# Retention by pairs of 64-token chunks, every product 64x64, in a kernel of retention and two mixtures of experts

## Chip, cores and metric

The kernel runs on one core of a Trainium2 chip. The metric is the device time of one execution in microseconds, a median of several runs. Engines are called as in the profile: PE is TensorE's matmul, PEld its weight load, DVE is VectorE, ACT ScalarE, POOL GpSimd, SP the queue that issues most DMAs.

## What is computed

Three layers. The first is retention over 4 sequences of 576 tokens with 8 heads of 64; the second a dense layer with softplus; the third a mixture of 8 experts, two per token.

```python
# q, k, v: (4, 8, 576, 64)
scores = scale * np.matmul(q, k.transpose(0, 1, 3, 2))
gamma = 1.0 - 2.0 ** (-5.0 - np.arange(H))
Dmat = np.where(rel >= 0, gamma[:, None, None] ** rel[None, :, :], 0.0)
ret = np.matmul(scores * Dmat, v)            # -> x: 2304 tokens x 512
h = x @ w_in                                 # 512 -> 2048
x = (np.maximum(h, 0) + np.log1p(np.exp(-np.abs(h)))) @ w_out
...
# top-2 gating over 8 experts, each 512 -> 1024 -> 512
```

## The kernel before

The 2304 tokens are cut into 18 chunks of 128 (C), of which 9 (PAIR) make two sequences; the fifth of nine straddles a border. Retention runs chunk by chunk (c), all in f32, from inputs that are laid out for it: `qk` has q and k with the head's dimension on the partitions (heads 2j and 2j+1 in the two halves, ROW), `kv` has k and v with the tokens on the partitions. For each chunk:

- `att_load` (L213) issues the DMAs of `qk` and `kv`, for the first ones also of the constants: `cm` (masks with decay, 512 KB), `ck` (decay for k), `CQ` (decay for q).
- `att_scale` (L226) multiplies k (L231) and q (L235) by their decay, on POOL but for chunk 0.
- `att_qk` (L237): eight products of 64x128x128 into two tiles `pa` (L243), one for each half of the rows of the array, and two multiplications by the mask on DVE (L247).
- `att_kv` (L252): eight products with 64 output rows (L262), and the new state on DVE, copied or added (L266, L268).
- `att_av` (L270): eight products with the old state (L281) and eight with the masked scores (L286) into one tile `px`; ACT writes its f16 part scaled into `x1` (L293), DVE the remainder (L294). Three chunks make a tile of 384 tokens for the next layer.

The dense layer takes f16 in two parts, three products for one. `g1` (L300) makes 128 columns of the hidden layer, 12 products of 128x384 (L306), evacuated by ACT (L315, L316) and softplus; `g2` (L325) multiplies by the second matrix (L337). Its weights come as f64: `decode` (L132) turns them into f32 on ACT (L141, L152) and DVE (L153, L155), `parts` (L159) splits them into two f16 parts on ACT (L161) and POOL (L162). 16 pieces are so treated.

The order of the work in the first part is a list written out by hand, `START` (L789): W is `warm` (products on a constant tile while the first inputs load), A load, S scale, Q, K, V the three attention steps, L a piece's load, a its decode, b its split, g one step of g1 or g2. The later chunks are put at steps of g1 by a small table (L769): loads 8 steps ahead of step g0, scaling 4 ahead, `att_qk` at g0, `att_kv` and `att_av` at g0+2. A scheduler then sets the order on every engine; each engine runs its own list in order.

In the same stage the experts' weights are read (L352, L354), split on ACT (L361) and DVE (L362) and written back to memory (L366), 64 pieces of 512 KB; each engine's list mixes them with the rest. After some 455 us follow the expert blocks (L683, L711), which the change does not touch.

## Time and profile before

| | |
|---|---|
| median of 3 runs | 912.62 us (911.99 to 914.01) |
| the profiled execution | 914.52 us, of which the profile's span is 912.3 us |
| PE busy | 885.7 us, 97% of the span |
| PEld, DVE, ACT, POOL busy | 50%, 72%, 42%, 29% |
| mean clock granted to PE | 0.988 of full |

The page gives busy time by engine, the span in 40 equal slices of 22.8 us with the busy share in tenths, the granted clock and the DMA's share and rate. Further views of the trace group instructions by line, list them in order of time, name who waited for whom, and give the busy time by stretch. A matmul on f32 stands in the trace as two passes, each with its own weight load, so eight written products count x16. A pass's own time is longer than the distance to the next, since passes overlap; what counts is the distance of starts.

### The profile page before, as it was taken

How to read it: one execution, taken by the hardware profiler on the slowest of the kernel's cores; microseconds unless marked ns; L12 is line 12 of the kernel's file. 1: busy time of each engine (PE TensorE's matmuls, PEld its weight loads, DVE VectorE, ACT ScalarE, POOL GpSimd, SP SyncE). 2: the span in 40 equal slices, each digit the busy share in tenths (PEclk: the TensorE clock that was granted, in tenths of full speed). 3: DMA queues.
4: the chain of work that ended last, by engine and by line, in shares of the span. 5: the costliest groups of instructions: out<-in, count | busy, mean ns of one | idle time of the engine just before them, and what ended most of it. 6: DMA issues, size and time to landing. Idle time of an engine off the chain costs nothing. (4 is left out here: it accounts for less than half of the span.)

```text
span 912.3 us, 17461 instructions
## 1 busy us (share of the span) xinstructions
PE 885.7 (97%) x5466; PEld 459.5 (50%) x5466; DVE 654.2 (72%) x1367; ACT 383.4 (42%) x595; POOL 260.5 (29%) x239
## 2 busy tenths in 40 slices
PE   7789999999999999999999999999999999999996
PEld 6554555555555555555544444444444444444442
DVE  4687866886887975434636789778887788878880
ACT  2589975775766674435432122221222212222120
POOL 1666642501410320110412423222232222321112
PEclk8899999999999999999999999999999999999998
DMA  9848999999999994003286875976357856875412
GB/s 352 318 170 271 296 283 394 384 318 351 388 336 342 376 403 121 1 1 70 67 242 128 139 122 101 240 189 156 66 152 176 208 126 163 246 178 157 116 24 35
DMA packets 141096, 187.11 MB, mean 205 GB/s; under 512 B 80016, under 2 KB 89232, under 8 KB 138960
## 3 DMA queue, kind: packets, MB, share of 16 engines
q1 hardware_dynamic: 130512, 164.90, 57.6%
q0 software_dynamic: 10496, 21.05, 11.8%
q8 instruction: 53, 0.87, 0.4%
q14 instruction: 35, 0.29, 0.1%
HBM read 246.01 MB, written 54.20 MB: 329 GB/s over the span
## 5 line engine op out<-in xcount | busy, mean ns | idle before, releaser
L702 DVE STREAM_TRANSPOSE ht<-hr 32x256 f32<-32x256 f32 x608 | 265.1, 436 | 11.7
L683 PE MATMUL ph<-w,xt 128*128 x984 | 218.9, 379 | 1.4 <-DMA xt<-xr 1.4
L711 PE MATMUL py<-w,ht 128*128 x984 | 218.6, 379 | 0.0
L306 PE MATMUL pg<-x,wi 128*128 128x384 f16 x1152 | 203.6, 326 | 2.7 <-POOL wi L162 1.9
L337 PE MATMUL p<-w,g 128*128 128x512 f16 x864 | 202.3, 381 | 1.7 <-POOL w L162 1.7
L306 PEld LDWEIGHTS <-wi 128*128 128x128 f16 x1152 | 111.4, 98 | 87.0 <-POOL wi L162 3.4
L683 PEld LDWEIGHTS <-xt 128*128 128x128 f16 x984 | 96.1, 98 | 117.2 <-DMA xt<-xr 1.6
L711 PEld LDWEIGHTS <-ht 128*128 128x128 f16 x984 | 96.3, 98 | 116.1
L723 POOL DMA_INDIRECT out_dram<-y,ti x41 | 64.9, 1583 | 279.0 <-ACT y L722 259.4
L337 PEld LDWEIGHTS <-g 128*128 128x128 f16 x864 | 82.6, 98 | 95.2 <-issue 6.2
L688 ACT ACTIVATE hr<-ph 128x512 f16<-128x512 f32 x82 | 60.0, 734 | 157.2 <-PE ph L683 150.4
L689 DVE SCALAR_TENSOR_TENSOR hr<-ph,hr 128x512 f16<-128x512 f32 x82 | 59.2, 727 | 66.3 <-ACT hr L688 65.2
L722 ACT ACTIVATE y<-py,ti 128x512 f32<-128x512 f32 x41 | 28.2, 687 | 180.4 <-PE py L711 180.4
L362 DVE SCALAR_TENSOR_TENSOR w<-w 128x1024 f16<-128x1024 f32 x64 | 79.0, 1236 | 32.4 <-ACT w L361 30.3
L320 DVE SCALAR_TENSOR_TENSOR r<-a,r 128x768 f32<-128x768 f32 x48 | 56.1, 1169 | 55.1 <-ACT a L319 54.2
L515 POOL DMA_INDIRECT table<-tb,pos x36 | 44.7, 1243 | 156.7 <-DVE pos L500 124.2
L361 ACT ACTIVATE w<-w 128x1024 f16<-128x1024 f32 x64 | 67.4, 1053 | 50.6 <-DMA w<-in_moe_w_dram 31.8
L315 ACT ACTIVATE r<-pg 128x384 f32<-128x384 f32 x96 | 46.7, 486 | 84.7 <-PE pg L306 84.6
L660 POOL DMA_INDIRECT xr<-X,ti x41 | 43.4, 1057 | 20.7 <-POOL ti L657 10.2
L316 ACT ACTIVATE a<-pg 128x384 f32<-128x384 f32 x96 | 46.6, 486 | 0.0
L318 ACT ACTIVATE a<-a 128x768 f32<-128x768 f32 x48 | 40.5, 843 | 1.1
L319 ACT ACTIVATE a<-a 128x768 f32<-128x768 f32 x48 | 40.3, 841 | 0.9
(132 smaller groups left out, 596.7 us busy)
## 6 DMA issues: line engine op xcount, KB each, us to landing
w<-wsc SPq DMA_DIRECT2D x78, 2048.0 KB
w<-in_moe_w_dram SPq DMA_DIRECT2D x64, 512.0 KB
wsc<-w SPq DMA_DIRECT2D x64, 512.0 KB
qk<-in_qk_dram SPq DMA_DIRECT2D x18, 512.0 KB
kv<-in_kv_dram SPq DMA_DIRECT2D x18, 512.0 KB
w<-in_moe_w_in_dram SPq DMA_DIRECT2D x8, 1024.0 KB
w<-in_moe_w_out_dram SPq DMA_DIRECT2D x8, 1024.0 KB
out_dram<-zero SPq DMA_DIRECT2D x1, 4608.0 KB
```

What stands on the lines that cost most here:

```text
L306: nc.tensor.matmul(pg, lhsT=wi[:, a, k, f * P:(f + 1) * P], rhs=x[:, b, k, :], start=n == 0, stop=n == 11)
L315: LAST["relu"] = nc.scalar.activation(r[:, i], pg, AF.Relu, scale=S_G / sx)
L320: nc.vector.scalar_tensor_tensor(out=r, in0=a, scalar=S_G, in1=r, op0=ALU.mult, op1=ALU.add)
L337: m = nc.tensor.matmul(PG[t, j], lhsT=g[:, a, f % 2, j * P:(j + 1) * P], rhs=wo[b][:, f, :], start=f == 0 and a + b == 0, stop=f == NFB - ...
L361: nc.scalar.activation(h[:, 0], t, AF.Copy, scale=s)
L362: nc.vector.scalar_tensor_tensor(out=h[:, 1], in0=t, scalar=s, in1=h[:, 0], op0=ALU.mult, op1=ALU.subtract)
L683: M1[i].append(nc.tensor.matmul(ph, lhsT=xt[:, a * 4 + k, :], rhs=AR[0][:, ds(r * 8192 + (b * 4096 + k * 1024 + n * 512), 512)], start=m = ...
L688: LAST["act"] = nc.scalar.activation(hi, ph, AF.Relu)
L689: nc.vector.scalar_tensor_tensor(out=lo, in0=ph, scalar=0.0, in1=hi, op0=ALU.max, op1=ALU.subtract)
L702: nc.vector.transpose(dst[32 * f:32 * f + 32, :, t], src[32 * t:32 * t + 32, :, f])
L711: M2[i].append(nc.tensor.matmul(py, lhsT=ht[:, c, :, a], rhs=AR[1][:, ds(r * 8192 + (b * 4096 + c * 512), 512)], start=len(M2[i]) == 0, st ...
L723: LAST["pool"] = nc.gpsimd.indirect_dma_start(out=out[:, :], out_offset=bass.IndirectOffsetOnAxis(ap=ti[:, 1:2], axis=0), in_=y[:, :], in_ ...
```

## The change

A chunk of 128 tokens is now a pair of 64-token chunks (x = 0, 1), nine of them to a sequence, so no chunk straddles a border. Every product is 64x64 with a contraction of 64, and uses a quarter of TensorE's array: rows `ROW[p]`, columns by where the output lies. The inputs are reordered on loading so that in each half of the partitions lies, for head half r, the chunk x = p ^ r. Decay moves: v is multiplied once by gamma to the minus position (`att_scale`, one operation), scores are only masked by a triangle of ones (one multiplication of 128x512, `tri`), states are plain sums, and the output is multiplied by gamma to the position, the scale and S_X1 (two multiplications into `f`, by `UP`). `f` lies in SBUF; ACT makes the f16 part from it, and the remainder is taken by DVE for the first three chunks and by POOL after.

`att_in` joins the scores and the two chunks' states in one group of up to 32 products; `att_out` the outputs, up to 32. Each group's products are issued together (`issue_after`). Both row halves of the array write to the one tile `pa`, and to the one tile `pst`, on different halves of the partitions. For each chunk DVE now has one mask, up to four state steps of 64x256 and two multiplications of 128x256. The constants are 68 KB (`cd`) ahead of the first `kv` and five pieces of `UP`, of up to 256 KB, one after each of the first five chunks. The warming is 22 products of 128x128 in place of 6 and 64 small ones.

```diff
@@ -49,31 +49,34 @@
...
+    up = g.T[None, :, None, :, None] ** (HALF * n[:, None, None, None, None] + t) * (S_X1 / np.sqrt(D))
...
+            down[p, :, :, r] = g[None, None, :, r] ** -(HALF * k[None, :, None] + t[:, None, None])
...
+        "c_down": np.concatenate([
+            np.tile(t[:, None] <= t[None, :], (2, 1)), down.reshape(P, PAIR * 8)], axis=1).astype(np.float32),
...
+    def units(a):
+        a = a.transpose(0, 2, 1, 3).reshape(NCH, 2, HALF, 4, 2, D)
+        return np.stack([np.stack([a[:, p ^ r, :, :, r] for r in range(2)], axis=1) for p in range(2)], axis=1)
...
@@ -186,113 +189,105 @@
     def warm(n):
         pw = ps.tile([C, 4, C], F32, tag="p2", name="pw", bufs=3)
-        for i in range(6):
+        for i in range(n):
             nc.tensor.matmul(pw[:, i % 4, :], lhsT=heat, rhs=heat, start=True, stop=True)
...
-            r, w = i // 2 % 2, HALF if i % 32 < 20 else C
-            nc.tensor.matmul(pw[r][ROW[i % 2], i // 4 % 4, :w], lhsT=heat[ROW[r], :64], rhs=heat[ROW[r], :w], start=True, stop=True)
...
+    UP = view(1, 12288, [PAIR, 4, HALF], F32)
+    cd = view(1, 29696, [HALF + PAIR * 8], F32)
+    tri, down = cd[:, :HALF], cd[:, HALF:].rearrange("p (n g) -> p n g", n=PAIR)
+    LD, AA, ST, X1 = {}, {}, {}, {}
+    def kinds(c):
+        return [(2 * c + x) % PAIR for x in range(2)]
     def att_load(c):
...
+        qk = ap.tile([P, 2, 8, HALF], F32, name="qk", bufs=3)
         nc.sync.dma_start(out=qk, in_=ins["qk"][c])
         if c == 0:
...
+            nc.sync.dma_start(out=cd, in_=ins["c_down"])
+        kv = ap.tile([P, 2, 8, D], F32, name="kv", bufs=3)
         nc.sync.dma_start(out=kv, in_=ins["kv"][c])
...
+        if c < 5:
+            n = 2 * c
+            m = min(n + 2, PAIR)
+            nc.sync.dma_start(out=UP[:, n:m], in_=ins["c_up"][:, n:m])
         LD[c] = (qk, kv)
     def att_scale(c):
         qk, kv = LD[c]
...
         e = nc.vector if c < 1 else nc.gpsimd
...
+        e.tensor_tensor(out=kv[:, 1], in0=kv[:, 1], in1=down[:, c % PAIR, :, None].to_broadcast([P, 8, D]), op=ALU.mult)
+    def att_in(c, tag="pa"):
         qk, kv = LD[c]
...
+        ka, kb = kinds(c)
+        pool, n = (ps, 3) if tag == "p2" else (ps1, 2)
+        pa = pool.tile([P, 8, HALF], F32, tag=tag, name="pa", bufs=n)
+        pst = pool.tile([P, 8, D], F32, tag=tag, name="pst", bufs=n)
+        use = (ka < PAIR - 1, kb < PAIR - 1)
+        with ExitStack() as tied:
+            for j in range(4):
+                for r in range(2):
+                    g = r * 4 + j
+                    for p in range(2):
+                        x = p ^ r
+                        if use[x]:
+                            m = nc.tensor.matmul(pst[ROW[1 - p], x * 4 + j], lhsT=kv[ROW[p], 0, g], rhs=kv[ROW[p], 1, g],
+                                                 start=True, stop=True)
+                            if LAST.get("in") != c:
+                                LAST["in"] = c
+                                tied.enter_context(tc.issue_after(m.ins))
+                        nc.tensor.matmul(pa[ROW[p], g], lhsT=qk[ROW[p], 1, g], rhs=qk[ROW[p], 0, g], start=True, stop=True)
+        a = AA[c] = ap.tile([P, 8, HALF], F32, name="a", bufs=2)
+        nc.vector.tensor_tensor(out=a, in0=pa, in1=tri[:, None, :].to_broadcast([P, 8, HALF]), op=ALU.mult)
+        sa = ST.get(2 * c)
+        for x in range(2):
+            if not use[x]:
+                continue
+            st = ST[2 * c + x + 1] = ring(("st", x), 1, 21504 + x * 2048, [4, D], F32, 2)
+            old = ST.get(2 * c + x)
             for r in range(2):
...
+                y = ROW[1 - r ^ x]
+                add = pst[y, 4 * x:4 * x + 4]
+                if (ka, kb)[x] == 0:
+                    nc.vector.tensor_copy(st[y], add)
+                else:
+                    nc.vector.tensor_tensor(out=st[y], in0=old[ROW[r ^ x]], in1=add, op=ALU.add)
+    def att_out(c, tag="pa"):
+        (qk, kv), a = LD.pop(c), AA.pop(c)
+        pool, m = (ps, 3) if tag == "p2" else (ps1, 2)
+        px = [pool.tile([P, 4, HALF], F32, tag=tag, name="px", bufs=m) for x in range(2)]
+        kk = kinds(c)
+        seen = set()
+        parts = [(True, j, 1 - x, r) for j in range(4) for x in range(2) for r in range(2) if kk[1 - x]]
+        mine = [(False, j, x, r) for j in range(4) for x in range(2) for r in range(2)]
+        with ExitStack() as tied:
+            both = parts + mine if kk[1] else mine + parts
+            end = {(x, r): n for n, (i, j, x, r) in enumerate(both)}
+            for n, (inter, j, x, r) in enumerate(both):
+                p, g = x ^ r, r * 4 + j
+                m = nc.tensor.matmul(px[x][ROW[r], j], lhsT=ST[2 * c + x][ROW[p], j] if inter else kv[ROW[p], 1, g],
+                                     rhs=qk[ROW[p], 0, g] if inter else a[ROW[p], g],
+                                     start=(x, r) not in seen, stop=end[x, r] == n, skip_group_check=True)
+                if not seen:
+                    tied.enter_context(tc.issue_after(m.ins))
+                seen.add((x, r))
+        f = ring("f", 1, 25600, [4, 2, HALF], F32, 2)
+        for x in range(2):
+            nc.vector.tensor_tensor(out=f[:, :, x], in0=px[x], in1=UP[:, kk[x]], op=ALU.mult)
         T, i = c // 3, c % 3
         if i == 0:
             X1[T] = mp1.tile([P, 2, KC, TT], F16, tag="x1", name="x1", bufs=2)
...
+        hi, lo = (X1[T][:, b, :, i * C:(i + 1) * C] for b in range(2))
+        f = f.rearrange("p j x t -> p j (x t)")
+        nc.scalar.activation(hi, f, AF.Copy)
+        e = nc.vector if c < 3 else nc.gpsimd
+        e.tensor_tensor(out=lo, in0=f, in1=hi, op=ALU.subtract)
     G, PG, X2R, LAST = {}, {}, {}, {}
@@ -770,9 +765,8 @@
         g0 = max({7: 22, 8: 27}.get(c, 0), (c // 3 - 1) * NS + (-1, 4, 9)[c % 3])
         at((1, max(12, g0 - 8)), att_load, c)
         at((1, max(16, g0 - 4)), att_scale, c)
-        at((1, g0), att_qk, c)
-        at((1, g0 + 2), att_kv, c)
-        at((1, g0 + 2), att_av, c)
+        at((1, g0), att_in, c)
+        at((1, g0 + 2), att_out, c)
     for t in range(NTILE - 1):
         at((2, (t + 1) * NS + 2), logits, t)
         at((2, (t + 1) * NS + (6 if t < NTILE - 2 else 3)), ranks, t)
@@ -787,9 +781,9 @@
     START = """
-        W64 A0 L A1 S0 Q0 K0 L A2 S1 V0 Q1 K1 a L A3 S2 V1 b Q2 K2 a L A4 S3 V2 b a L b g g
-        Q3 K3 a L A5 S4 V3 b g g a L b g g Q4 K4 a L S5 V4 b g g Q5 K5 a L V5 L b g g a L b g g
-        a L b g g a L b g g a L b g A6 g a L b g g a L b g g S6 a b g g Q6 a b g K6 g a V6 b r
+        W6 W16 A0 L A1 S0 Q0  L A2 S1 V0 Q1  a L A3 S2 V1 b Q2  a L A4 S3 V2 b a L b g g
+        Q3  a L A5 S4 V3 b g g a L b g g Q4  a L S5 V4 b g g Q5  a L V5 L b g g a L b g g
+        a L b g g a L b g g a L b g A6 g a L b g g a L b g g S6 a b g g Q6 a b g  g a V6 b r
         g g g g
     """.split()
     PA, PB = 2, 2
@@ -828,8 +822,8 @@
             piece(s)
         else:
             c = int(s[1:])
-            f = {"A": att_load, "S": att_scale, "Q": att_qk, "K": att_kv, "V": att_av, "W": warm}[s[0]]
-            f(c, "p2") if s[0] in "KV" and c < 3 else f(c)
+            f = {"A": att_load, "S": att_scale, "Q": att_in, "V": att_out, "W": warm}[s[0]]
+            f(c, "p2") if s[0] == "V" and c < 3 else f(c)
     while order:
         step()
     for g in sorted(todo):
```

On PE the list shows chunk 16's two groups, between the wide products of `g1` (L306 before, L301 now). Before, the scores, and later the state and output:

```order
L306 MATMUL pg<-x_2754,wi 128x384
L243 MATMUL pa<-qk 128x128 x8
L306 LDWEIGHTS wi
```

```order
L306 MATMUL pg<-x_2754,wi 128x384
L262 MATMUL pst<-kv 64x64 x8
L281 MATMUL px<-w_85 64x128 x8
L286 MATMUL px<-a,kv 64x128 x8
L442 LDWEIGHTS w_85
```

Now (L239 the states, L244 the scores in turn, 16 of each; then L274 the output, with the old state and with the scores):

```order
L301 MATMUL pg<-x_3112,wi 128x384
L239 MATMUL pst<-kv 64x64
L244 MATMUL pa<-qk 64x64
L239 MATMUL pst<-kv 64x64
L244 MATMUL pa<-qk 64x64
```

```order
L301 MATMUL pg<-x_3112,wi 128x384
L274 MATMUL px<-qk,w_85 64x64 x16
L274 MATMUL px<-a,kv 64x64 x16
L437 LDWEIGHTS w_85
```

The state's products have moved from the second group into the first, between the scores.

On ACT the first rows of the program, before (L141 and L152 decode, L161 the first f16 part of a piece, L293 a chunk's output into `x1`):

```order
L141 ACTIVATE w_84<-w_84 128x1024
L152 ACTIVATE low<-w_84 128x512
L293 ACTIVATE x_246<-px 128x4x128
L152 ACTIVATE low<-w_84 128x512
L293 ACTIVATE x_246<-px 128x4x128
L141 ACTIVATE w_84<-w_84 128x1024
L152 ACTIVATE low<-w_84 128x512
L161 ACTIVATE wi<-w_85 128x4x256
L152 ACTIVATE low<-w_84 128x512
L293 ACTIVATE x_246<-px 128x4x128
L161 ACTIVATE wi<-w_85 128x4x256
```

Now (L144, L155, L164 and L288 in the same roles):

```order
L144 ACTIVATE w_84<-w_84 128x1024
L155 ACTIVATE low<-w_84 128x512 x2
L288 ACTIVATE x_225<-w_85 128x4x128
L164 ACTIVATE wi<-w_85 128x4x256
L144 ACTIVATE w_84<-w_84 128x1024
L155 ACTIVATE low<-w_84 128x512 x2
L288 ACTIVATE x_225<-w_85 128x4x128
L164 ACTIVATE wi<-w_85 128x4x256
L144 ACTIVATE w_84<-w_84 128x1024
L155 ACTIVATE low<-w_84 128x512 x2
L288 ACTIVATE x_225<-w_85 128x4x128
L164 ACTIVATE wi<-w_85 128x4x256
```

The first two pieces' f16 parts now each stand ahead of the next chunk's output, where both stood behind the second and the third; three pieces are decoded before the first wide product where it was two.

## Rows read from the trace of the kernel before

**Rows 1.** The page: PE's busy time, and its busy tenths by slice.
```profile
PE 885.7 (97%) x5466; PEld 459.5 (50%) x5466; DVE 654.2 (72%) x1367; ACT 383.4 (42%) x595; POOL 260.5 (29%) x239
...
PE   7789999999999999999999999999999999999996
```

**Rows 2.** Busy time by stretch: us; PE, PEld, DVE, ACT, POOL; clock, DMA share, GB/s.
```profile
33.00:107.00 74.00, 67.76 (x502) 38.10 (x501) 57.36 (x83) 66.51 (x103) 49.57 (x32) 0.98 0.73 236
105.00:245.00 140.00, 140.00 (x1057) 80.06 (x1056) 108.77 (x182) 95.16 (x151) 42.63 (x27) 1.00 1.04 353
245.00:345.00 100.00, 100.00 (x758) 57.56 (x757) 79.31 (x120) 68.67 (x105) 22.75 (x19) 1.00 1.01 360
345.00:450.00 105.00, 105.00 (x716) 58.24 (x714) 49.24 (x144) 46.54 (x87) 12.89 (x13) 1.00 0.17 41
```

**Rows 3.** ACT's waits from 105 to 345 us: total us, times, longest.
```profile
ACT w L361 <- DMA w<-in_moe_w_dram: 31.8, 23, 4.9
ACT r L315 <- PE pg L306: 21.9, 23, 3.2
ACT w L361 <- DMA wsc<-w: 17.2, 12, 6.1
```

**Rows 4.** PE in order of time, chunk 16: start us, us from first start to last end.
```profile
352.12 1.16 PE L243 MATMUL pa<-qk 64*128 64x128 f32 x16
353.21 2.12 PE L306 MATMUL pg<-x,wi 128*128 128x384 f16 x12
...
361.10 0.69 PE L262 MATMUL pst<-kv 128*64 128x64 f32 x16
361.62 1.05 PE L281 MATMUL px<-w 128*64 128x128 f32 x16
362.49 1.04 PE L286 MATMUL px<-a,kv 128*64 128x128 f32 x16
363.47 1.06 PE L442 MATMUL lg<-wg,w 128*128 128x16 f16 x36
```

**Rows 5.** Busy time by stretch, as rows 2: the warming's quarter passes, the start.
```profile
6.20:6.23 0.03, 0.03 (x12) 0.03 (x8) 0.00 (x0) 0.00 (x0) 0.00 (x0) 1.00 1.10 426
6.20:6.70 0.50, 0.50 (x44) 0.50 (x40) 0.00 (x0) 0.00 (x0) 0.00 (x0) 1.00 1.02 351
12.70:19.50 6.80, 6.70 (x58) 5.95 (x60) 3.87 (x8) 1.13 (x2) 2.27 (x2) 0.50 1.04 396
27.20:32.70 5.50, 4.79 (x48) 4.31 (x49) 1.52 (x3) 0.56 (x2) 1.16 (x1) 0.50 1.03 395
```

**Rows 6.** Line 194's passes from 6.35 to 6.70 us: ns shortest/median/longest, first, last start.
```profile
L194 PE MATMUL pw<-heat x36: 218/218/218, 6.2 to 6.7; 64*64 64x64 f32 x36
```

**Rows 7.** DVE in order of time, the start.
```profile
10.96 0.85 DVE L266 COPY w<-pst 64x256 f32<-64x256 f32 x2
...
32.77 0.69 DVE L294 SCALAR_TENSOR_TENSOR x<-px,x 128x512 f16<-128x512 f32 x1 [2.85 <-ACT x L293]
35.26 1.29 DVE L153 SCALAR_TENSOR_TENSOR low<-w,low 128x512 int32<-128x512 int32 x2 [1.79 <-ACT low L152]
```

**Rows 8.** POOL in order of time, the start, and chunk 16's scaling.
```profile
14.09 1.04 POOL L231 TENSOR_TENSOR kv<-kv,ck 128x512 f32<-128x512 f32 x1 [11.03 <-DMA kv<-in_kv_dram]
15.09 1.27 POOL L235 TENSOR_TENSOR w<-qk,w 128x512 f32<-128x512 f32 x1
24.00 2.13 POOL L162 TENSOR_TENSOR wi<-w,wi 128x1024 f16<-128x1024 f32 x1 [7.65 <-ACT wi L161]
...
296.39 1.19 POOL L231 TENSOR_TENSOR kv<-kv,ck 128x512 f32<-128x512 f32 x1 [6.65 <-DMA kv<-in_kv_dram]
```

**Rows 9.** PE in order of time, the warming.
```profile
1.15 2.93 PE L190 MATMUL pw<-heat 128*128 128x128 f32 x12 [1.15 <-DVE heat L91]
4.01 3.52 PE L194 MATMUL pw<-heat 64*64 64x64 f32 x128
```

**Rows 10.** ACT in order of time, the third piece's f16 part.
```profile
38.05 1.06 ACT L161 ACTIVATE wi<-w 128x1024 f16<-128x1024 f32 x1
```

More of the change, by code (lines that the diff above doesn't have):

```diff
@@ L227, in att_scale @@
         qk, kv = LD[c]
-        u = c % PAIR
         e = nc.vector if c < 1 else nc.gpsimd
-        if u < PAIR - 1:
-            e.tensor_tensor(out=kv[:, 0], in0=kv[:, 0], in1=ck[:, kind(c), :, None].to_broadcast([C, H, D]), op=ALU.mult)
-        if u:
-            n = HALF if u == 4 else C
-            QS[c] = ring("qs", 1, 24576, [4, C], F32, 2)
-            e.tensor_tensor(out=QS[c][:, :, :n], in0=qk[:, 0, :, :n], in1=CQ[kind(c)][:, :, :n], op=ALU.mult)
-    def att_qk(c):
-        qk, kv = LD[c]
-        pa = [ps1.tile([C, 4, C], F32, tag="pa", name="pa", bufs=2) for g in range(2)]
-        for j in range(4):
-            for g in range(2):
-                nc.tensor.matmul(pa[g][:, j, :], lhsT=qk[ROW[g], 1, j, :], rhs=qk[ROW[g], 0, j, :], start=True, stop=True)
-        AA[c] = []
-        for g in range(2):
-            a = ap.tile([C, 4, C], F32, name="a", bufs=2)
-            nc.vector.tensor_tensor(out=a, in0=pa[g], in1=cm[:, g], op=ALU.mult)
-            if c % PAIR == 4:
-                nc.gpsimd.memset(a[:HALF, :, HALF:], 0.0)
-            AA[c].append(a)
@@ L252, in att_kv @@
-    def att_kv(c, tag="pa"):
-        qk, kv = LD[c]
-        u = c % PAIR
-        if u == PAIR - 1:
-            return
-        pst = ps.tile([P, 4, D], F32, tag=tag, name="pst", bufs=3) if tag == "p2" else \
-            ps1.tile([P, 4, D], F32, tag="pa", name="pst", bufs=2)
-        for j in range(4):
-            for r in range(2):
-                nc.tensor.matmul(pst[ROW[r], j], lhsT=kv[:, 0, 2 * j + r], rhs=kv[:, 1, 2 * j + r], start=True, stop=True)
-        st = ST[c + 1] = STZ[c % 2]
-        for r in range(2):
-            if u in (0, 4):
-                nc.vector.tensor_copy(st[ROW[r], r], pst[ROW[r]])
-            else:
-                nc.vector.tensor_tensor(out=st[ROW[r], r], in0=ST[c][ROW[r], r], in1=pst[ROW[r]], op=ALU.add)
@@ L270, in att_av @@
-    def att_av(c, tag="pa"):
-        (qk, kv), qs, a = LD.pop(c), QS.pop(c, None), AA.pop(c)
-        u = c % PAIR
-        px = ps.tile([P, KC, C], F32, tag=tag, name="px", bufs=3) if tag == "p2" else \
-            ps1.tile([P, KC, C], F32, tag="pa", name="px", bufs=2)
-        n, last, w = 0, 15 if u else 7, HALF if u == 4 else C
-        for j in range(4 if u else 0):
-            for r in range(2):
-                nc.tensor.matmul(px[ROW[r], j, :w], lhsT=ST[c][:, r, j], rhs=qs[:, j, :w], start=n < 2, stop=False,
-                                 skip_group_check=True)
-                n += 1
-        for j in range(4):
-            for r in range(2):
-                nc.tensor.matmul(px[ROW[r], j, :], lhsT=kv[:, 1, 2 * j + r], rhs=a[r][:, j], start=n < 2, stop=n >= last - 1,
-                                 skip_group_check=True)
-                n += 1
+        e.tensor_tensor(out=kv[:, 1], in0=kv[:, 1], in1=down[:, c % PAIR, :, None].to_broadcast([P, 8, D]), op=ALU.mult)
@@ new lines, in att_in @@
+    def att_in(c, tag="pa"):
+        qk, kv = LD[c]
+        ka, kb = kinds(c)
[5 more added lines that the diff above has]
+            for j in range(4):
+                for r in range(2):
+                    g = r * 4 + j
+                    for p in range(2):
+                        x = p ^ r
[14 more added lines that the diff above has]
+            old = ST.get(2 * c + x)
+            for r in range(2):
+                y = ROW[1 - r ^ x]
[4 more added lines that the diff above has]
+                    nc.vector.tensor_tensor(out=st[y], in0=old[ROW[r ^ x]], in1=add, op=ALU.add)
@@ L291, in att_av @@
             X1[T] = mp1.tile([P, 2, KC, TT], F16, tag="x1", name="x1", bufs=2)
-        x = X1[T]
-        nc.scalar.activation(x[:, 0, :, i * C:(i + 1) * C], px, AF.Copy, scale=S_X1)
-        nc.vector.scalar_tensor_tensor(out=x[:, 1, :, i * C:(i + 1) * C], in0=px, scalar=S_X1,
-                                       in1=x[:, 0, :, i * C:(i + 1) * C], op0=ALU.mult, op1=ALU.subtract)
+        hi, lo = (X1[T][:, b, :, i * C:(i + 1) * C] for b in range(2))
[3 more added lines that the diff above has]
+        e.tensor_tensor(out=lo, in0=f, in1=hi, op=ALU.subtract)
     G, PG, X2R, LAST = {}, {}, {}, {}
```

44 lines of the change are left out of this document (9 added, 35 removed).

## Prediction

> **What bounds the kernel now.** I read the page's head first [rows 1]: TensorE (PE) is busy for 97% of the span, so what shortens PE's work should shorten the kernel, unless something else is nearly as full. It holds stage by stage. In the slices PE is below nine tenths only in the first three and in the last one. The table of stretches [rows 2] splits what lies between: from 105 to 345 us PE is never idle, but the DMA queues are just as full (share 1.04 and 1.01, 353 and 360 GB/s); from 345 to 450 PE is full and the DMA at 0.17. From 33 to 107 PE has 67.8 of 74 us, and ACT 66.5: while the first layer's weights are decoded, two engines are nearly full. ACT's waits in the middle stretch [rows 3] say what the DMA does there: the splitting of the second layer's weights (L361) stands still for 31.8 us on loads and 17.2 us on stores, in front of the activations that PE's products wait for; PE has so far always had enough buffered. So: a start bound by chains of waits, a decode stage bound by ACT and PE, a stage in which PE is the bound with the DMA right behind it, and PE alone after that.
>
> **The retention on PE, per chunk.** Chunk 16 shows the old price [rows 4]: scores from 352.12 to the next line's 353.21, 1.09 us; state and output from 361.10 to 363.47, 2.37 us, of which the state takes 0.52 (361.10 to 361.62) and the product with the old state 0.87. Sum 3.46 us. Each written product is two passes in the trace (eight give x16). The new code has 32 products of 64x64 in each of two groups, 64 passes each. The trace of before has this very shape in its warming: over a stretch of 0.47 us with a pass long 0.218 us, the table counts 44 passes where its first 0.03 us counts 12, so 32 passes start in 0.47 us, **14.6 ns** a pass [rows 5, 6]; the quarters are used in turn there as here. A group then takes 63 x 14.6 ns and one pass's own 0.218 us until the wide products go on: 1.14 us. Two groups: 2.28 us, **1.18 us less** per full chunk. Upper bound for a pass: the state's rows, 16 in 0.52 us, 33 ns, where only two parts of the array work side by side; lower bound half of 14.6, as no row shows passes nearer. I take 14.6, since array shape, width and alternation are the same.
>
> After 105 us lie chunks 7 to 17. Seven are full: 8.3. Chunks 8 and 17 make no state (2.94 before): 0.66 each. Chunk 9 reads none (2.59): 0.3. Chunk 13 multiplies half as many columns by the old state (3.03): 0.75. Together **10.6 us**, 8.8 of them before 345 us and 1.8 behind it.
>
> **How much of the 8.8 arrives.** The bytes of that stage do not change (the new chunk loads are as large; only the constants shrink, early on). 240 us at some 356 GB/s must fit into 231 us: 371 GB/s. Where the queues are full without a break, at the start, the rows show 395 and 396 [rows 5]. It fits on average, at 94% instead of 90%. But ACT stands still on DMA for 49 us of 240 already, and at these places PE's lead is used up first. Bounds: nothing lost, or all 8.8. I take a third, 2.9, off: 5.9 arrive.
>
> **The other engines in that stage.** DVE loses one masking product of 0.68 us and the remainder (0.69), and gets two additions of 64x256 (0.42 each) and two half products of the output with the decay (bounded by the same 0.42 from below and 0.68 from above): 0.3 to 0.8 us a chunk, 3 to 9 us in 188 of 240 us busy [rows 2, 7]; hidden, as PE is never idle and so no wait of PE for DVE stands in that stage. POOL swaps the scaling of q (1.27 us) for the remainder, of half the size of the decode's 2.13 us, 1.07: about equal [rows 8]. ACT's evacuation has the same size. The first group now waits for POOL's scaled values where the old scores did not. That is hidden: scaled values lie ready tens of us ahead (chunk 16's at 297.6, its scores at 352.12 [rows 4, 8]).
>
> **The start.** Warming: 22 products of 128 instead of 6 and 64 small ones. Six took 2.86 us (from 1.15 to 4.01) [rows 9], so 22 take 10.5 us if the clock stays low and half of that if it were high throughout: they end between 6.4 and 11.6. Either way chunk 1 comes later: its values landed at 14.09 [rows 8], and with 0.46 MB less of mask constants and 0.26 MB of output decay ahead of them some 0.2 MB earlier, 0.5 us at 396 GB/s: 13.6. The clock: from 12.7 to 19.5 and from 27.2 to 32.7 it is at the lower level, 0.50 (1.2 GHz) [rows 5], after PE had stood idle; the new groups leave more gaps, so I take 0.50 throughout, doubling a group to 2.1 us. From there, with the pitches of DVE's rows (0.6 us for 128x512, 0.42 for 64x256) [rows 7]:
> - POOL scales until 14.6; group one until 16.7; mask and two state steps, 1.5: 18.2; group two until 20.3; two products with the decay, 0.85: 21.2; behind them stand two pairs of decode steps and a remainder, 3.0: 24.2.
> - Chunk 2's group one is long done; mask and state 1.5: 25.7; group two: 27.8; products 0.85: 28.7; two decode steps and the remainder, 1.85: **30.5**.
>
> Only then does the first layer have both parts of its input. Before, the remainder ended at 33.46 [rows 7]: 2.9 us won. It would be 6 more if the clock stayed high. On ACT the order moves too: the first decoded piece now goes ahead of chunk 1's evacuation (the order shows it), and the third piece, at 38.05 before [rows 10], follows at about 30.5 + 1.2 = 31.7: **6 us** earlier. In the decode stage ACT is 90% busy, so 6 us of ACT's lead last to its end if nothing else binds; PE, with 2.9 and four chunks of 1.18, is ahead by 7.6. The smaller holds: 6 us. Bounds: 2.9 (PE's lead alone, chunks swallowed by waits) and 10 (clock up early, and idle gaps closing).
>
> **Sum.** 6 + 5.9 + 1.8 = 13.7 us. The profiled execution took 914.5 us (span 912.3), 1.9 above the median of 912.62; 914.5 less 13.7 is 900.8, and at the level of the median **898.9**. After 450 us nothing changes; that part moves earlier as a whole.
>
> **Rivals.**
> - *The DMA holds the middle.* Splitting, loads and stores keep their pace, and PE, faster, waits for ACT behind L361. For it: share 1.0 and ACT's 49 us. Against it: ACT also waited 21.9 us for PE in the same stretch [rows 3], so the DMA was not the pace everywhere. Then 6 + 1.8 arrive: 904.8.
> - *Everything arrives.* The clock rises early in the start (10) and the DMA gives way (8.8 + 1.8): 892.
> - *The halves take turns, and it is slower.* In the new groups the upper and the lower half of the array's rows write one bank of PSUM (`pa`, and `pst`) in the same moment, on different partitions; in the old warming, and in the old scores, each row half had a bank of its own, so no row shows this pattern. If the halves have to take turns, a pass costs 29.2 ns, a group 2.06 us, a full chunk 4.1 instead of 3.46. It decides from 24 ns a pass on, where two groups cost as much as the old chunk. Loss after 105 us: seven at 0.66, and some 2.7 for the four others, 7.3 us. The start's chain gets four groups longer by 1.9 us at the low clock, which takes its gain: 920. For it: even with separate banks the old scores' two row halves took 68 ns a pass (16 in 1.09 us), so halves do not always run freely side by side. Against it: within a bank they write different partitions.
>
> The Trainium skill (TensorEngine Tiling (Array Packing), section "Gotcha 1: PSUM Pressure") says that different row tiles cannot access the same PSUM bank simultaneously and that software must see to it; by that rule this rival would be the forecast. Its page PSUM — Partial Sum Buffer (section "PSUM bank collisions raise a hardware error") says of two engines that different quadrants of one bank run clean. No row here shows either.
>
> **How the numbers follow.** Forecast 0.55 (its own range 894 to 905: the start giving between 2.9 and 9, the DMA taking between a sixth and two thirds); DMA holds 0.20; everything 0.12; turns 0.13. What a measurement can tell from no change is 0.2%, 1.8 us. The first three are faster, with 0.02 taken off for starts that lose what PE gains; in the fourth a little falls within 0.2%. Faster 0.85, same 0.03, slower 0.12. The range from 890 to 907 takes in the first three and leaves out the fourth with the tails.
>
> **What would show it.** Right: 64 passes of a group starting within about 0.93 us between 105 and 450 us, a group about 1.1 us from its first start to the next line's; the first wide product near 30 us; the third decoded piece near 32 us; PE idle of a few us in all between 105 and 345 us, named as waiting for ACT behind L361 or for its chain. Wrong: passes at 29 ns (turns); ACT behind L361 waiting on the DMA as long as before while PE stands idle some 9 us (DMA); first wide products after 33 us.

## The result, and the profile after

The changed kernel takes **919.73 us** (918.38 to 921.6, 4 runs) against 912.33 for the kernel before, measured beside it: ratio 1.0079, 95% interval 1.0057 to 1.0101. It is slower by 0.8%; 898.9 was predicted. The profiled execution took 919.36 us.

The page's head, and below it the table of stretches (columns as in [rows 2]), which answer to [rows 1, 2]:

```profile
PE 878.6 (96%) x6458; PEld 450.7 (49%) x6458; DVE 668.8 (73%) x1402; ACT 383.7 (42%) x595; POOL 256.1 (28%) x232
...
PE   7878999999999999899999999999999999999996
```

```profile
33.00:107.00 74.00, 64.37 (x674) 36.21 (x673) 58.31 (x87) 63.92 (x99) 44.70 (x27) 0.95 0.75 253
105.00:345.00 240.00, 233.73 (x2377) 130.87 (x2376) 193.30 (x313) 163.04 (x253) 64.36 (x45) 0.99 1.00 350
345.00:450.00 105.00, 101.62 (x822) 55.45 (x821) 49.49 (x130) 45.56 (x85) 14.94 (x15) 0.98 0.15 35
```

PE is busy 7 us less, and the kernel is longer: from 105 to 345 us PE stands idle for 6.3 us where it was never idle, from 345 to 450 for 3.4, and its clock is below full in both stretches. What PE waited for, over the span (us in total, times, longest):

```profile
PE px L274 <- DVE w L259: 10.7, 9, 2.0
...
PE px L274 <- issue: 2.6, 5, 1.1
```

The first row is the second group of a chunk (L274) waiting for the state additions on DVE (L259); in the last, "issue" means that nothing in the trace explains the wait.

The passes themselves came as forecast. PE in order of time, chunk 16, to be held against [rows 4]:

```profile
351.02 0.27 PE L239 MATMUL pst<-kv 64*64 64x64 f32 x1
...
352.11 2.12 PE L301 MATMUL pg<-x,wi 128*128 128x384 f16 x12
...
360.00 0.69 PE L274 MATMUL px<-qk,w 64*64 64x64 f32 x32
360.52 0.65 PE L274 MATMUL px<-a,kv 64*64 64x64 f32 x32
361.10 1.06 PE L437 MATMUL lg<-wg,w 128*128 128x16 f16 x36
```

The groups take 1.09 and 1.10 us, 2.19 against 3.46 before. So PE does its work faster and then stands. To see where the time is lost, I count `g1`'s passes (12 to a step of the first layer) and take the start of the first one of a step, in us, in each profiled execution; the last three columns are experiments of the next section:

| step | before | changed | prio | prioall | rank3 |
|---|---|---|---|---|---|
| 0 | 32.8 | 28.6 | 29.0 | 29.0 | 29.5 |
| 6 | 62.8 | 54.9 | 54.9 | 53.1 | 55.2 |
| 12 | 91.8 | 90.6 | 90.6 | 88.4 | 90.9 |
| 66 | 342.3 | 341.2 | 335.0 | 333.7 | 335.2 |
| 78 | 396.9 | 399.7 | 395.3 | 393.9 | 387.6 |
| 90 | 444.7 | 447.5 | 443.1 | 441.7 | 435.5 |
| end of span | 912.3 | 917.5 | 912.2 | 907.7 | 902.5 |

The changed kernel leads by 4.2 us at the start and 7.9 at step 6, by 1.2 at step 12, by 1.1 at step 66, and is 2.8 us behind at step 78. Three places, then: steps 6 to 12, the middle stage, where the 8.8 us that PE's work was forecast to shrink by left no trace, and steps 66 to 78. Behind step 90 another 2.4 us go (2.8 us behind there, 5.2 at the end).

**The middle stage.** DVE in order of time around chunk 14, whose first group had ended at 300.8:

```profile
304.75 1.23 DVE L357 SCALAR_TENSOR_TENSOR w<-w 128x1024 f16<-128x1024 f32 x1 [0.25 <-ACT w L356]
306.01 0.42 DVE L259 TENSOR_TENSOR w<-w,pst 64x256 f32<-64x256 f32 x1
306.47 0.69 DVE L246 TENSOR_TENSOR a<-pa,w 128x512 f32<-128x512 f32 x1
307.26 0.96 DVE L315 SCALAR_TENSOR_TENSOR r<-a,r 128x768 f32<-128x768 f32 x1
308.25 0.41 DVE L259 TENSOR_TENSOR w<-w,pst 64x256 f32<-64x256 f32 x1
308.70 0.56 DVE L316 CAST g<-r 128x768 f16<-128x768 f32 x1
309.29 0.42 DVE L259 TENSOR_TENSOR w<-w,pst 64x256 f32<-64x256 f32 x1
309.72 0.96 DVE L318 TENSOR_TENSOR g<-r,g 128x768 f16<-128x768 f32 x1
310.69 0.42 DVE L259 TENSOR_TENSOR w<-w,pst 64x256 f32<-64x256 f32 x1
```

and PE at the same time:

```profile
308.88 0.33 PE L274 MATMUL px<-qk,w 64*64 64x64 f32 x4
311.17 0.62 PE L274 MATMUL px<-qk,w 64*64 64x64 f32 x26 [1.95 <-DVE w L259]
```

The four additions are 1.7 us of work, spread over 5.1 us of DVE's list among the softplus (L315, L316, L318), behind a splitting (L357) that itself waits for ACT. The second group reads the state after the chunk's first half, and writes its `px` into the two buffers that `pa` and `pst` held, so it cannot finish before the last addition. Between 110 and 375 us PE's waits for these additions add up to 5.9 of 6.3 us of idle time.

**Steps 66 to 78.** PE in chunk 17's second group, and the clock of the stretch behind it (columns as in [rows 2]):

```profile
383.42 0.41 PE L274 MATMUL px<-a,kv 64*64 64x64 f32 x13
384.25 0.34 PE L274 MATMUL px<-a,kv 64*64 64x64 f32 x4 [0.41 <-issue]
384.98 0.34 PE L274 MATMUL px<-a,kv 64*64 64x64 f32 x4 [0.39 <-issue]
385.71 0.36 PE L274 MATMUL px<-a,kv 64*64 64x64 f32 x6 [0.40 <-issue]
387.15 0.36 PE L274 MATMUL px<-a,kv 64*64 64x64 f32 x5 [1.08 <-issue]
388.60 3.46 PE L332 MATMUL p<-w,g 128*128 128x512 f16 x9 [1.10 <-issue]
```

```profile
388.00:391.40 3.40, 2.80 (x7) 0.98 (x7) 1.09 (x3) 0.30 (x1) 0.93 (x1) 0.50 0.02 1
```

A group that should take 1.1 us takes 5.7 (382.91 to 388.60), from 384.25 us on in bursts of four to six passes, 0.73 or 1.45 us apart, and then the clock is granted at its lower level (0.50, 1.2 GHz), so that nine wide passes take 3.46 us instead of 2.1.

### The profile page after: what moved, and what is told of

Read it like the earlier page. It is cut to its first block, busy times and chain, and to the rows that moved or that the text cites. A ratio compares the mean times of both kernels' runs of the same rounds, so it can differ in the third digit from the quotient of the medians.

```text
span 917.5 us, 19458 instructions
## 1 busy us (share of the span) xinstructions
PE 878.6 (96%) x6458; PEld 450.7 (49%) x6458; DVE 668.8 (73%) x1402; ACT 383.7 (42%) x595; POOL 256.1 (28%) x232
## 5 line engine op out<-in xcount | busy, mean ns | idle before, releaser
L332 PE MATMUL p<-w,g 128*128 128x512 f16 x864 | 204.9, 384 | 7.7 <-POOL w L165 5.3
L301 PE MATMUL pg<-x,wi 128*128 128x384 f16 x1152 | 204.7, 328 | 1.8 <-ACT x L288 1.3
L301 PEld LDWEIGHTS <-wi 128*128 128x128 f16 x1152 | 111.9, 98 | 85.6 <-issue 2.9
L357 DVE SCALAR_TENSOR_TENSOR w<-w 128x1024 f16<-128x1024 f32 x64 | 83.8, 1320 | 36.7 <-ACT w L356 31.2
L684 DVE SCALAR_TENSOR_TENSOR hr<-ph,hr 128x512 f16<-128x512 f32 x82 | 59.4, 728 | 67.7 <-ACT hr L683 66.0
L315 DVE SCALAR_TENSOR_TENSOR r<-a,r 128x768 f32<-128x768 f32 x48 | 54.7, 1140 | 50.7 <-ACT a L314 50.0
L510 POOL DMA_INDIRECT table<-tb,pos x36 | 40.8, 1135 | 140.3 <-DVE pos L495 100.4
L290 POOL TENSOR_TENSOR x<-w,x 128x512 f16<-128x512 f32 x15 | 20.8, 1385 | 116.6 <-ACT x L288 73.9
L313 ACT ACTIVATE a<-a 128x768 f32<-128x768 f32 x48 | 40.4, 842 | 1.1
```

The lines of the kernel that those rows point to most:

```text
L301: nc.tensor.matmul(pg, lhsT=wi[:, a, k, f * P:(f + 1) * P], rhs=x[:, b, k, :], start=n == 0, stop=n == 11)
L315: nc.vector.scalar_tensor_tensor(out=r, in0=a, scalar=S_G, in1=r, op0=ALU.mult, op1=ALU.add)
L332: m = nc.tensor.matmul(PG[t, j], lhsT=g[:, a, f % 2, j * P:(j + 1) * P], rhs=wo[b][:, f, :], start=f == 0 and a + b == 0, stop=f == NFB - ...
L357: nc.vector.scalar_tensor_tensor(out=h[:, 1], in0=t, scalar=s, in1=h[:, 0], op0=ALU.mult, op1=ALU.subtract)
L684: nc.vector.scalar_tensor_tensor(out=lo, in0=ph, scalar=0.0, in1=hi, op0=ALU.max, op1=ALU.subtract)
```

## The experiments

All of them change the changed kernel, but for `warm22`, which changes the kernel before. Ratios are to the kernel before on the same chip.

**again.** No edit.

> The changed kernel unchanged, once more. It tells whether the stall in chunk 17's second group (383.8 to 388.6 us: bursts of 4 to 6 passes with 0.4 to 1.1 us between them that no wait explains, then a wide group at half clock; about 5 us) belongs to this program or to that one execution. If it belongs to the program, the stall stands at the same place in this profile and the median stays near 919.7 us. If it was a chance of that execution, the profiled execution is near 914.5 us and the median of many runs lies below 919.

918.46 us, ratio 1.0055 (1.0042 to 1.0068). The stall is there again in chunk 17's second group: gaps of 0.41, 0.39, 0.38, 1.09, 0.24 and 0.45 us from 384.7 on. It belongs to the program.

**late.**

```diff
-        at((1, g0 + 2), att_out, c)
+        at((1, g0 + 4), att_out, c)
```

> From chunk 7 on the second group (L274) stands four steps of the wide products behind the first one, instead of two; same work on every engine. Theory (the second group now waits for DVE's state additions L259, which stand in DVE's list among the splitting and the remainders): PE's idle of 6.2 us between 110 and 375 us nearly goes (under 1.5 us), and with it the fall of the clock at 237.8 to 241.2 (1.7 us): 919.7 less 6 to 8, 912 to 914 us. Rival (the DMA holds the middle stage): the idle time moves to the wide products, behind ACT L356's waits for loads, and the time stays within 2 us of 919.7. Rival (DVE simply has too much work there): the additions come as much later as the group does, and idle and time stay.

921.01 us (915.84 to 923.73), ratio 1.0093 (1.0077 to 1.0108): no gain, though not one wait for L259 is left after 110 us. PE's waits there:

```profile
PE pst L239 <- DVE w L282: 5.2, 3, 2.6
PE pg L301 <- ACT a L311: 2.5, 1, 2.5
```

PE's idle time between 110 and 375 us is 10.1 us, more than before the edit. The second group now stands one or two steps ahead of the next chunk's first group, which takes over the two PSUM buffers and must wait until DVE has read them (L282). No expectation had this: moving the group changes which of DVE's results is late. (Chunk 17's group ran at 394.2, after the stall's time, in 0.94 us.)

**prio.** The mask and the additions of chunks 7 to 17 go first in DVE's list:

```diff
-        nc.vector.tensor_tensor(out=a, in0=pa, in1=tri...
+        with tc.high_priority() if c > 6 else ExitStack():
+            nc.vector.tensor_tensor(out=a, in0=pa, in1=tri...
...
```

> The masking product (L246) and the state additions (L259) of chunks 7 to 17 are put ahead of other work in DVE's list; place of the groups and work unchanged. Theory (order of DVE's list decides): the additions stand right behind the mask, PE's waits for L259 go from 9 us to under 2, 912 to 914 us, as in the run with the later second group. Rival (DVE is late altogether): additions early make the wide products' other inputs (L316, L318) late instead; PE idles as much behind those, 918 to 920 us.

914.1 us (12 runs), ratio 1.0008 (0.9997 to 1.0019). DVE around chunk 14 (the mask is L247 in this kernel), and PE's waits after 110 us:

```profile
303.47 0.43 DVE L259 TENSOR_TENSOR w<-w,pst 64x256 f32<-64x256 f32 x1
303.92 0.69 DVE L247 TENSOR_TENSOR a<-pa,w 128x512 f32<-128x512 f32 x1
304.65 1.20 DVE L259 TENSOR_TENSOR w<-w,pst 64x256 f32<-64x256 f32 x3
```

```profile
PE px L274 <- DVE w L259: 0.8, 2, 0.5
```

The additions stand together around the mask, PE's idle time between 110 and 375 us falls from 6.3 to 2.3 us, and from step 12 to 66 it takes 244.4 us where both other kernels took 250.5 and 250.6. The theory holds, and with it the DMA rival falls: PE gets 6.1 of 8.8 us with the queues as full as in the changed kernel (share 1.00 from 105 to 345 us, 351 GB/s against 350). The stall in chunk 17 stays (5.66 us from first to last start).

**prioall.** The same for the chunks of the decode stage:

```diff
-        with tc.high_priority() if c > 6 else ExitStack():
+        with tc.high_priority() if c > 2 else ExitStack():
```

> As the run before, and the same for chunks 3 to 6, in the decode stage. Theory (in 50 to 70 us the lead of the start is lost because the mask stands on DVE behind L315, which waits 2.6 us for ACT, so PE idles, its clock falls at 60.3 to 67.1 us and ACT's decoding stands still for 3 us): the lead at step 12 (90.6 us in the changed kernel) grows by 2 to 4 us, and the time is 908 to 911 us. Rival (the decode chain on ACT and POOL is the pace there whatever DVE's order): step 12 stays at 90 to 91 us and the time is that of the run before.

911.71 us (11 runs), ratio 0.9984 (0.9969 to 0.9999). Step 12 came at 88.4 us here, but the later kernels below, alike up to there, had 90.9, 88.7, 89.6 and 90.0 against 90.2 to 90.9 in the four executions without this edit: about 1 us, not 2 to 4. The starts differ too: counted from step 0 it is 59.4 to 59.7 us in four of the five and 61.4 in the other, against 61.6 to 62.0. The medians differ by 2.4 us (914.1 and 911.71), so the time is not the rival's either. But PE still stood for 5.4 us at 55.2, waiting for the additions on DVE. A gain of some 2 us; its theory is not shown.

**warm22.** The kernel before, with the new warming:

```diff
-        for i in range(6):
+        for i in range(n):
...
-            nc.tensor.matmul(pw[r][ROW[i % 2], i // 4 % 4, :w], lhsT=heat[ROW[r], :64], ...
...
-        W64 A0 L A1 S0 Q0 K0 L A2 ...
+        W6 W16 A0 L A1 S0 Q0 K0 L A2 ...
```

> The kernel before with the change's warming alone (22 products of 128x128 for 6 of them and 64 small ones). It tells what that part is worth by itself: theory, nothing that can be measured (912 to 914 us), since the chain from the chunk loads on sets the start; rival, the longer warming keeps the clock up or delays the first chunks, and the first wide product, at 32.8 us before, moves by over 1 us and the time with it.

909.3 us, ratio 0.9954 (0.9937 to 0.9970), 4.4 us below the kernel before: the rival. The first wide product comes at 28.9 us as in the changed kernel, and the clock from 12.5 to 20 us is full where [rows 5] had 0.50:

```profile
12.50:20.00 7.50, 4.50 (x77) 3.77 (x74) 5.78 (x10) 3.17 (x5) 2.27 (x2) 1.00 1.04 392
```

**oldwarm.** The changed kernel with the old `warm` (that diff turned round) and

```diff
-        W6 W16 A0 L A1 S0 Q0  L A2 ...
+        W64 A0 L A1 S0 Q0  L A2 ...
```

> The changed kernel with the warming of the kernel before (6 products of 128x128 and 64 small ones). The new warming alone, in the kernel before, brought the first wide product from 32.8 to 28.9 us and 4.4 us of time. Theory (all that the changed kernel wins in the start is its warming): the first wide product comes at 31 to 33 us instead of 28.6, and the time is 921 to 925 us. Rival (the new groups shorten the chain of the start by themselves, as the prediction had it): it stays at 28 to 30 us, and the time at 918 to 920 us.

919.99 us, ratio 1.0075 (1.0061 to 1.0090). The first wide product comes at 31.6 us, so of 4.2 us won there the warming has 3 and the new groups 1.2; but the time does not move. Yet the start's gain is still there at step 90, which comes at 450.8 us here and at 447.5 in the changed kernel, 3.3 us earlier. The difference is made up behind `g1`: from its last pass to the end of the span it takes 445.0 us here and 448.8 there, with a wait for transposed rows of 0.7 against 2.0 us and no fall of the clock behind it. No run shows what decides that part, so from this run the warming's worth in time stays open.

**rank3.** prioall, and the fourth tile's `ranks` four steps later. This step ends in six indirect DMAs, which POOL issues (L510): they write rows of a table to addresses that come from data.

```diff
-        at((2, (t + 1) * NS + (6 if t < NTILE - 2 else 3)), ranks, t)
+        at((2, (t + 1) * NS + (10 if t == 3 else 6 if t < NTILE - 2 else 3)), ranks, t)
```

> The run prioall with one more edit: the ranks of the fourth tile, whose six indirect DMAs on POOL (L510) ran from 373.7 to 381 us, right through chunk 17's second group (375.4), go four steps later. Theory (the unexplained gaps in that group come only where POOL issues those DMAs and PE runs short products at the same time): chunk 17's second group takes 0.94 us as the undisturbed ones do, the clock does not fall there, and 3.5 to 4.5 us of gaps and 3.4 us of half clock are saved: 911.7 less 5 to 8, 904 to 907 us. Rival (the gaps belong to that place of PE's program, its instructions being fetched late there): the second group of chunk 17 stalls as before, 911 to 912 us.

**903.63 us** (903.0 to 904.22), ratio 0.9889 (0.9873 to 0.9906): 8.1 us below prioall's median, at the edge of the 904 to 907 expected. Chunk 17's second group is whole, and POOL's DMAs begin 16 us behind it:

```profile
376.75 0.69 PE L274 MATMUL px<-qk,w 64*64 64x64 f32 x32
377.26 0.65 PE L274 MATMUL px<-a,kv 64*64 64x64 f32 x32
```

```profile
393.08 1.00 POOL L510 DMA_INDIRECT table<-tb,pos  x1 [11.60 <-DVE pos L495]
```

**meet14.** rank3, and:

```diff
-        at((1, g0 + 2), att_out, c)
+        at((1, g0 + (5 if c == 14 else 2)), att_out, c)
```

> As rank3, and chunk 14's second group goes three steps later, from 303.6 to about 316 us, into the third tile's six indirect DMAs on POOL (311.9 to 319.5 us in the run prioall). Theory (short products and POOL's indirect DMAs at the same time): the gaps of 0.4 to 1.1 us without a wait that explains them now stand in chunk 14's second group, which takes 3 us or more. Rival (place in the program): it takes 0.94 us. The time is of no interest; the wide products behind it may wait for the input it gives.

908.75 us (0.9947, 0.9928 to 0.9967). Chunk 14's group met the DMAs and did not stall:

```profile
314.50 0.69 PE L274 MATMUL px<-qk,w 64*64 64x64 f32 x32
315.02 0.65 PE L274 MATMUL px<-a,kv 64*64 64x64 f32 x32
```

```profile
313.42 1.83 POOL L510 DMA_INDIRECT table<-tb,pos  x1 [0.30 <-issue]
315.55 1.79 POOL L510 DMA_INDIRECT table<-tb,pos  x1 [0.30 <-issue]
```

So the DMAs are not enough for a stall. In this stage of full queues they stood 2.1 us apart, where chunk 17 met them every 1.28 us. But neither that distance nor the place of chunk 17 decides: chunk 8's second group ran beside the first tile's DMAs in eleven of the profiled executions, and in seven of them (the changed kernel, again, prio, prioall, dmaonly, dmaonly2, rank3old) it took 1.68 to 2.29 us from first to last start, with gaps that no wait explains; in the other four (oldwarm, rank3, meet14, ein) 0.94. In again, whose DMAs began at 169.45 and 170.73 us:

```profile
170.69 0.37 PE L274 MATMUL px<-a,kv 64*64 64x64 f32 x5 [0.33 <-issue]
171.45 0.50 PE L274 MATMUL px<-a,kv 64*64 64x64 f32 x14 [0.39 <-issue]
```

**dmaonly.** prioall, with the DMAs of `ranks` in a function of their own:

```diff
+        at((2, (t + 1) * NS + 10), scatter, t, pos, tb) if t == 3 else scatter(t, pos, tb)
+    def scatter(t, pos, tb):
         for j in range(3):
```

> The run prioall with only the six indirect DMAs of the fourth tile's table (on POOL) four steps later; its rank products on PE and DVE's work for them stay where they are (rank3 moved those too, and meet14 showed chunk 14's second group meeting the third tile's six DMAs without a stall). Theory (the DMAs are needed for the stall): chunk 17's second group takes 0.94 us and the time is 903 to 906 us, as rank3. Rival (the stall hangs on the place of PE's instructions, which rank3 shifted by the rank products): the stall is back, 3.5 to 4.5 us of gaps and a fall of the clock, 910 to 912 us.

913.12 us (12 runs, 909.95 to 918.03), ratio 1.0000 (0.9984 to 1.0015), with the stall. But the edit did not do what it said: POOL had nothing else to do and began the DMAs at 373.68 us all the same. Nothing follows.

**dmaonly2.** dmaonly, and in `scatter` the DMAs' data are made to depend on chunk 17's output:

```diff
+        if t == 3:
+            late = X1[5][:, 0, 0, 2 * C:2 * C + 6].rearrange("p (j k) -> p j k", k=2)
+            nc.gpsimd.tensor_scalar(tb[:, :, :, 2], late, 0.0, None, op0=ALU.mult)
```

> The run dmaonly left the six DMAs where they were (they began at 373.7 us, as in prioall), since POOL issues them as soon as their positions are there. Here their data depend on chunk 17's output (one column of zeros is made from it on POOL), so that they cannot begin before its second group has ended; the order of PE's instructions is that of prioall, row for row. Theory (those DMAs are needed for the stall): chunk 17's second group takes 0.94 us, no fall of the clock there, 903 to 906 us, as rank3. Rival (the place of PE's instructions makes the stall): it stays, 910 to 913 us.

906.21 us (903.66 to 907.0), ratio 0.9921 (0.9906 to 0.9936). With PE's instructions in the same order the stall is gone:

```profile
377.00 0.69 PE L274 MATMUL px<-qk,w 64*64 64x64 f32 x32
377.51 0.65 PE L274 MATMUL px<-a,kv 64*64 64x64 f32 x32
```

```profile
382.54 1.51 POOL L516 DMA_INDIRECT table<-tb,pos  x1 [0.28 <-POOL tb L513]
```

The DMAs are needed for it; the place of PE's instructions alone does not make it. Nor does a load of instructions fit: in oldwarm the one beside that group (16 KB on the trace's instruction queue) begins at 391.1 us, and four of the five gaps lie ahead of it (386.8 to 390.2 us).

**ein.** rank3, and in the hand-written order:

```diff
-        Q3  a L A5 S4 V3 b g g a L b g g Q4  a L S5 V4 b g g Q5  a L V5 L b g g a L b g g
+        Q3  a L A5 S4 V3 b g g a L b Q4 g g S5 a L V4 b Q5 g g a L V5 L b g g a L b g g
```

> As rank3, and in the decode stage the first groups of chunks 4 and 5 stand two wide steps earlier in the program, and chunk 5's scaling earlier, so that the mask of chunk 4 does not stand on DVE behind L315, which waits for ACT. Theory (that mask's place makes PE idle 5.4 us at 55.2 in prioall, its clock fall for 6.8 us, and ACT wait 3 us): the idle time at 55 us falls below 2 us, step 12 of the wide products comes at 85 to 87 us instead of 88.4, and the time is 1.5 to 3 us below rank3's. Rival (ACT and POOL set the pace of the decode stage, and PE only waits elsewhere): step 12 stays within 1 us of 88.4, time within 1 us of rank3's.

902.48 us (901.63 to 907.91), ratio 0.9882 (0.9865 to 0.9898), not to be told from rank3. The profiled execution is the longest of the five, 907.91 us. (The mask that stood at 55 us is chunk 5's; its first group was moved too.) PE is not idle from 50 to 60 us any more, but stands for 2.7 us in the next ten:

```profile
50.00:60.00 10.00, 10.00 (x158) 6.16 (x154) 8.71 (x13) 7.57 (x12) 5.09 (x4) 1.00 0.62 209
60.00:70.00 10.00, 7.31 (x38) 3.33 (x35) 8.88 (x14) 7.99 (x14) 7.28 (x5) 1.00 0.71 251
```

Step 12 comes at 89.1 us, inside the spread of the kernels that it should beat. That fits the rival, by which the decoding sets the pace; a gain of a microsecond stays possible.

**rank3old.** rank3 with the edit of oldwarm.

> rank3 with the warming of the kernel before. In the changed kernel the old warming moved the first wide product from 28.6 to 31.6 us and the time not at all (919.99 against 919.73), in the kernel before the new warming gained 4.4. Theory (what the start wins is kept where nothing later takes it back): 3 to 4.5 us slower than rank3's 903.6, 906.5 to 908. Rival (the decode stage takes it back, as ACT and POOL set its pace): within 1 us of 903.6.

905.88 us (902.71 to 911.56), ratio 0.9936 (0.9911 to 0.9961). By the medians it is 2.3 us above rank3, between the two expectations; by the two ratios 0.47%, 4.3 us, as its eight runs lie in two groups (902.71 to 905.89, and 910.33 to 911.56). Step 0 is 1.7 us later than rank3's, step 90 2.7. What the start wins is kept here up to step 90, as it was in oldwarm.

## Why the prediction was wrong

The forecast was a lead of 13.7 us; the changed kernel's profiled execution is 5.2 us behind the one before, 18.9 us off. By the table of steps 4.8 us of that are lost up to step 12 (1.2 us of lead instead of 6), 6.0 from there to step 66 (nothing instead of 5.9), 5.7 from there to step 90 (3.9 lost instead of 1.8 won) and 2.4 behind it.

- **The passes: right.** 14.6 ns a pass was taken from the warming; chunk 16's groups took 1.09 and 1.10 us against 1.14 forecast.
- **"Hidden, as PE is never idle and so no wait of PE for DVE stands in that stage": the first step that failed.** I priced DVE's part by its busy time, 3 to 9 us beside 52 us of idle (5.2 us more were measured from 105 to 345 us), and did not ask where in DVE's list the new steps stand and who waits for them. Before, the group at g0+2 needed from DVE the masks alone; its old state was a chunk old. Now the state after the chunk's first half is made between its own two groups, four more steps of DVE that PE waits for, two wide steps after the first group. That there was no such wait before only told that the old distance was enough for the old work. Cost: 5.9 us of waits, and 1.7 for a clock at its lower level from 237.9 to 241.2 us. prio shows it: the order of DVE's list alone is worth 4.4 us (again's 918.46 less 914.1, in one series).
- **"5.9 arrive": right in size once that wait is gone** (6.1 in prio, with 2.3 us of idle left), nothing in the changed kernel. But the reason is not shown: the third was taken off for the DMA, and though ACT stood 33 us on loads and 22 on stores in prio, of PE's 2.3 us of idle only 0.6 waited for ACT; 0.8 still waited for the additions, 0.4 are chunk 8's unexplained gap. That the size fits is luck. The rival in which the DMA takes all is false.
- **The 1.8 us behind 345 us: lost to something that no row of before showed.** Chunk 17's stall cost 3.4 us of gaps and 1.7 of clock in the changed kernel; by prioall and rank3 it is worth 8.1. In the kernel before, chunk 17's old products (385.3 to 387.1 us) stood in the midst of the same six DMAs without a gap. Without the stall the term is right: rank3 wins 2.1 us from step 66 to step 90.
- **The start: right time, half the reason.** The first wide product came at 28.6 us (30.5 forecast) and the third piece's f16 part at 30.93 (31.7), and the clock was at the lower level from 16 to 33 us, nearly as assumed. But the gain is the warming's for the greater part: 3.0 of 4.2 us by oldwarm, and 3.9 in the kernel before (warm22). I had asked of the warming only when it ends, and not what it does to the clock that [rows 5] shows behind it.
- **"6 us of ACT's lead last to its end if nothing else binds": the second step that failed.** In busy time from the span's start ACT's lead was 3.9 us at 40 us (18.73 against 14.79), not 6; the order of its steps had only brought one piece forward. From 50 to 70 us ACT then worked 13.88 us against 16.59 before. PE, ahead by 7.9 us, waits three times: 1.3 and 1.8 us for weights that ACT and POOL are still decoding, and 1.9 us for the state additions on DVE, which stand there behind a step (L315) that waits for ACT:

```profile
58.31 0.38 PE L332 MATMUL p<-w,g 128*128 128x512 f16 x1 [1.31 <-ACT w L164]
60.52 0.59 PE L332 MATMUL p<-w,g 128*128 128x512 f16 x1 [1.83 <-POOL w L165]
62.95 0.44 PE L274 MATMUL px<-qk,w 64*64 64x64 f32 x2 [1.85 <-DVE w L259]
```

PE's clock falls for 6.7 us, and 1.2 us of lead are left at step 12:

```profile
60.40:67.10 6.70, 4.73 (x68) 3.17 (x68) 5.36 (x11) 2.66 (x5) 2.75 (x3) 0.50 1.01 372
```

In the kernels with prioall's edit and the new warming it is 0.9 to 3.4; this is the part of the forecast that no experiment brought back, and its cause is not shown.

- **The rival "the halves take turns": false, though its 920 lies beside the result.** `pa` and `pst` are written by both row halves in turns, at the warming's pitch; no undisturbed group of 64 has its passes 29 ns apart. The Trainium skill's rule that different row tiles cannot access one PSUM bank simultaneously (TensorEngine Tiling (Array Packing), Gotcha 1: PSUM Pressure) costs nothing here: the first group's 64 passes and the way to the next line take 1.09 us, with both row halves on one tile. The right direction by the wrong mechanism: by this rival the loss was to be in PE's busy time, and PE is busy 7 us less.
- **"After 450 us nothing changes"**: from the last pass of `g1` to the end of the span it takes 448.8 us after 446.3. In the changed kernel a wait for transposed rows at 490 us lasts 2.0 us (1.4 before), and the clock stands at its lower level from 493.8 to 497.2 us. Whether the change has a part in it is not shown: in the 14 profiles of this study this stretch is 444.7 to 449.1 us, with a wait of 0.7 to 2.3 us, and in six of the twelve with the new groups it is 444.7 to 445.7, below the 446.3 of the kernel before.

Put right, the change does what it was costed for in kind: rank3 is 1.1% faster than the kernel before (0.9873 to 0.9906), some 10 us of the 13.7 forecast, and some 16 us below the change as it was made (919.73 and 903.63). By the table its lead is 0.9 us at step 12 (6 forecast), 6.2 more by step 66 (5.9) and 2.1 more by step 90 (1.8). Part of it is the warming's: without that (rank3old) the ratio is 0.9936.

## What to carry to other kernels

When a shorter step on the bound engine also splits its work in two with another engine in between, look up where that engine's steps stand in its own list and what they wait behind: a share of busy time says nothing about that. An engine that never waited before has only shown that the old distances were enough; and a lead of one engine is worth what the next one has done in work, not what one of its steps has moved. When something moves the time and no wait explains it, look at what the other engines issue in that very stretch, and move that by a true dependency: a later place in the program may not move it at all (dmaonly).

## What the runs showed of the hardware

- Short f32 products on quarters of the array, with both row halves writing one tile of PSUM, run at the pitch of the warming: 64 passes of the second group start within 0.94 us, 14.9 ns apart. They come in rounds some 58 ns apart, four passes to a round. Fewer passes save nothing: the undisturbed groups of 48 (in chunks 8, 9, 13 and 17) take 0.93 to 0.94 us as well, and so does each half of chunk 6's second group, which was issued in two parts (108.51 and 110.78 us) of 32 passes, two to a round.
- A stall of PE without a wait. In all six profiled executions in which chunk 17's second group ran beside the six indirect DMAs on POOL (the changed kernel, again, prio, prioall, dmaonly, oldwarm) it took 4.38 to 5.68 us from first to last start; in the six where these DMAs ran at another time (late, rank3, meet14, ein, dmaonly2, rank3old) 0.94. Chunk 8's stalled for 0.7 to 1.4 us beside the first tile's DMAs in seven of eleven, chunk 14's did not beside the third tile's (meet14), and the old 64x128 products of chunk 17 did not either. What it is of PE that the DMAs hold up stays open.
- Two microseconds of idle time can cost more than themselves: after 2.0 us of idle time at 234.4 to 236.8 us the changed kernel's clock was granted at 0.50 for 3.4 us. The same kind of gap at 309.2 us (1.95 us) left it at full, while in again 2.35 us of idle time between 308.8 and 311.5 us were followed by the lower level from 313.0 to 316.4 us.
- 22 products of 128x128 while the first inputs load, in place of 6 and 64 small ones, kept the clock at 1.00 from 12.5 to 20 us where it had been 0.50, and took 4.4 us off the kernel before (warm22).
